# More zero products in the first chain, and other slots for the side units, in a kernel of memory attention followed by a bilinear layer

## The chip, the cores and the metric

The kernel runs on one core of a Trainium2 chip. The metric is the device time of one execution in microseconds (us); the time of a kernel is the median of several executions. Engines are named as in the profile: PE is TensorE, DVE is VectorE, ACT is ScalarE, POOL is GpSimd, SP is SyncE. L337 is line 337 of the kernel.

## What is computed

```python
a   = softmax(phi, axis=seq)                      # (8, 8, 576, 32): batch, heads, seq, memory slots
k_m = einsum('bhsm,bhsd->bhmd', a, k)             # q, k, v: (8, 8, 576, 64)
v_m = einsum('bhsm,bhsd->bhmd', a, v)
attn = softmax(q @ k_m.T / sqrt(64), axis=slots)
x   = (attn @ v_m), heads side by side            # (4608 tokens, 512)
out = ((x @ w_a) * (x @ w_b)) @ w_out             # w_a, w_b: (512, 1536), w_out: (1536, 512)
```

## The kernel before

The eight batches are eight periods of 576 tokens. For each period the kernel folds the memory values into the weights: `vab` holds v_m times w_a and v_m times w_b, for the 8 x 32 memory slots of the heads and the 1536 columns, so that the up projection is one matmul of the attention weights A with `vab`.

A period is made of **side units** and of **up steps**. The side units are made by `units` (L187) and named by short strings:

- `exp0`, `exp1`: exponentials of phi on ACT (L195)
- `qt0` to `qt3`: transposes of q on DVE (L204)
- `ks0`, `ks1`, `vs0`, `vs1`: sums over tokens on PE in tiles of 64 rows and 32 columns (`pk`, L256), then a reciprocal and a scaling on DVE (`kvm`); `kv` and `km` are the same for all at once in later periods (`pkv`, L213; `rep`, L233)
- `kt`, `vt`, `kvt`: transposes on PE and a copy to `kvT` on DVE
- `s0`, `s1`, `sc`: scores on PE (`pscore`, L292); `e0`, `e1`: their exponential E on ACT (L305)
- `den0`, `den1`: denominators on PE (`pD`, L314) and a logarithm on ACT; `nr0`, `nr1`: R on ACT and A = E x R on DVE, from period 3 on on POOL (L325)
- `v0a` to `v2b`: a fold of 512 columns, n = 0, 1, 2, with `w_a` (a) or `w_b` (b) on PE (`pva`, L337); `x0a` to `x2b`: its copies from PSUM, one half on ACT and one on DVE (L349); `hv`, `hx`: the same for 256 columns
- `L`: the four loads of a later period, issued on POOL's queue

An up step is one of 12 blocks of 128 of the 1536 columns: the products `pa` (L584), a copy on ACT (`a_sb`, L587), the products `pb` (L594), and the product `ht` on DVE (L597). A step over both token halves gives a slot after its pa and one after its pb; a half step gives one slot. `ups` (L600) takes the next entry of a list of slots after each. Step i needs only the columns 128 i to 128 i + 127 of `vab`, so steps 8 to 11 alone need the folds v2a and v2b.

The down projection is `po` (L389) for the first four blocks of 128 tokens, which the letters y and a number pull out of `early_downs`, and one level of a Strassen-like scheme after that: `two_downs` (L453) on PE, with sums of ht made on POOL (`h_sums`, L444) and sums of `w_out` (`w_sums`, L429). `Work.advance` spreads these products over the slots by a planned rate.

Periods 0 and 1 begin with a hand-written order, `chain` (L651), which also takes `f` and a number: that many products of zeros of 256 columns (`fill`, L147, into the tile `pw`). The schedule is manual: each engine takes its instructions in the order in which the code issues them. Ahead of everything `fill(16)` runs 16 products of zeros of 512 columns.

The loads are issued on POOL's queue in the order of the code: q, k and v of period 0, then `w_a` and `w_b` in pairs of columns 0 to 256, 256 to 512, 512 to 1024 and 1024 to 1536 (L98), then `w_out`, with the inputs of period 1 between its parts.

Of the kernel before, what the change touches and what calls it, by code (L numbers as in the profile page):

```python
# [18 lines left out]
def kernel(  # L19
# [72 lines left out]
    def load(b):  # L92
        load_phi(b)
        load_k(b)
        load_v(b)
        load_q(b)
# [50 lines left out]
    def fill(n, cols=512):  # L147

        pw = banks.tile([P, 512], F32, name="pw")
        for _ in range(n):  # L150
            nc.tensor.matmul(pw[:, :cols], warm[:, :P], warm[:, :cols], start=True, stop=True)
# [273 lines left out]
    def sum_weights():  # L425
        t = [w_sums[:, x] for x in range(4)]
        for out, in0, in1 in ((t[0], quarter(0, 1), quarter(0, 0)), (t[1], quarter(1, 1), t[0]),
                              (t[2], quarter(1, 1), quarter(0, 1)), (t[3], quarter(1, 0), t[1])):
            nc.gpsimd.tensor_tensor(out=out, in0=in0, in1=in1, op=ALU.subtract)  # L429
# [146 lines left out]
    def up(b, i, hfs):  # L576
        A, vab = attn[b], vabs[b]
        base = S * (b % 2)
        fs = slice(P * i, P * (i + 1))
        a_sbs = []  # L580
        for hf in hfs:
            pa = banks.tile([P, HALF], F32, name="pa")
            for g in range(2):
                nc.tensor.matmul(pa, vab[0][:, g, fs], A[:, g, HALF * hf:HALF * (hf + 1)],  # L584
                                 start=(g == 0), stop=(g == 1))
            a_sb = apool.tile([P, HALF], F16, name="a_sb")
            nc.scalar.copy(out=a_sb, in_=pa)  # L587
            a_sbs.append(a_sb)
        if len(hfs) > 1:
            yield  # L590
        for hf in hfs:
            pb = banks.tile([P, HALF], F32, name="pb")
            for g in range(2):
                nc.tensor.matmul(pb, vab[1][:, g, fs], A[:, g, HALF * hf:HALF * (hf + 1)],  # L594
                                 start=(g == 0), stop=(g == 1))
            t0 = base + HALF * hf
            nc.vector.tensor_tensor(out=ht[:, i, t0:t0 + HALF], in0=a_sbs[hf - hfs[0]], in1=pb, op=ALU.mult)  # L597
        yield

    def ups(steps, side=()):  # L600

        side = iter(side)
        for step in steps:
            for _ in up(*step):
                work.advance()
                next(side, us[step[0]]["-"])()
        for f in side:
            work.advance()
            f()

    def steps(b, lo, hi):

        return [(b, i, (0, 1)) for i in range(lo, hi)]

    def half_steps(b, hf, lo=0):

        return [(b, i, (hf,)) for i in range(lo, NFF)]
# [10 lines left out]
    def slots(b, names):  # L628

        def both(fs):  # L630
            return lambda: [f() for f in fs]
        def unit(n):
            if n == "fin":
                return lambda: work.pull(-work.done % NFF)
            if n == "L":
                return lambda: load(b + 2) if b + 2 < B else None
            if n[0] == "y":
                return lambda: some(int(n[1:]))
            if n[0] == "d" and n[1:].isdigit():
                return lambda: work.pull(int(n[1:]))  # L640
            return us[b + n.endswith("'") - n.endswith("_")][n.rstrip("'_")]

        return [both([unit(n) for n in x.split("+")]) for x in names.split()]
# [3 lines left out]
    def some(n):  # L647
        for _ in range(n):
            next(early, None)

    def chain(b, plan):  # L651


        for x in plan.split():
            if x[0] == "f":
                fill(int(x[1:]), 256)
            elif x[0] == "y":
                some(int(x[1:]))
            else:
                us[b][x]()  # L660

    fill(16)
    chain(0, "exp0 exp1 ks0 kt0 qt0 qt1 f2 s0 e0 ks1 kt1 den0 qt2 qt3 f2 s1 nr0 e1 vs0 vs1 den1 vt0 vt1 nr10 nr11 hv0a hx0a")
    ups(steps(0, 0, 4), slots(0, "hv0b+hx0b hv1a+hx1a - hv1b+hx1b - v1a+x1a - v1b+x1b"))
    load(2)
    ups(steps(0, 4, 12), slots(0, "- - - - v2a+x2a+v2b+x2b - -"))
    chain(1, "exp0 exp1 y9 ks0 y3 kt0 qt0 qt1 y1 y3 ks1 qt2 s0 e0 y6 kt1 qt3 den0 y3 s1 nr0 e1 y4 y2 den1 vs0 vs1 vt0 y1 vt1 nr1 hv0a hx0a hv0b y3 hx0b y2")
    load(3)
    sum_weights()
    ups(steps(1, 0, 4), slots(1, "- hv1a+hx1a hv1b+hx1b+y1 - v1a+x1a y3+v1b x1b y3"))  # L670
    ups(half_steps(1, 0, 4), slots(1, "- v2a+x2a+v2b+x2b+qt0' - - qt1'+exp0'+qt2' exp1' - kv'+km'+y9"))
    work.plan(S + HALF, 10)
    ups(half_steps(1, 1, 4), slots(2, "- kvt qt3 sc+e0+e1+den0 - nr0+den1+v0+x0a - - x0b+nr1 - v1+x1b x1a"))
    second = "v2_+x2a_+exp0 x2b_ exp1 - qt0+kv+km - qt1+qt2 kvt+qt3 sc+e0 - e1+v0+x0a den0+x0b v1+x1a nr0+L x1b+exp0' den1 - nr1+v2+x2a - x2b+exp1' - qt0'+kv'+qt1' km' - qt2'+kvt'+qt3'"
    every = "- sc+e0 e1 den0 v0+x0a+x0b - - nr0+exp0' - - v1+x1a qt0' x1b+den1 exp1' - v2+x2a+x2b nr1+qt1' kv'+km' qt2' - qt3' - kvt'+L -"
    last = "sc+e0 - e1 - v0+x0b - x0a den1 - - den0 v1+x1b x1a+nr0 - - - - nr1+v2+x2a - - - - - x2b"
    for b in range(2, B):
        if b == 2:
            load(4)
# [35 lines left out]
```

The softmax here doesn't subtract the row's maximum and nothing guards it: scores larger than these inputs give would overflow.

## Time and profile before

| What | Value |
|---|---|
| Median of 6 runs | 247.74 us (246.92 to 247.94) |
| Profiled execution, time | 247.71 us |
| Profiled execution, span | 246.0 us |
| PE busy | 232.8 us, 95% |
| DVE, ACT, POOL busy | 168.5, 158.7, 152.9 us |
| Mean granted clock of PE | 0.986 |
| DMA on POOL's queue | 22.71 MB |

The span runs from the first to the last instruction of the program; the time of the execution has 1.7 us more around it. The chain of work that ended last is followed back from the last instruction, at each step to what released it. A busy PE is not PE at its peak: its matmuls are pipelined, and the end of each is modelled, so the step from one start to the next says more than the length of one. The granted clock is 1.00 at full speed. The notation [0.36 <-DMA x] behind an instruction is the idle time of its engine ahead of it, and what ended it.

### The profile page before, as it was taken

How to read it: one execution, taken by the hardware profiler on the slowest of the kernel's cores; microseconds unless marked ns; L12 is line 12 of the kernel's file. 1: busy time of each engine (PE TensorE's matmuls, PEld its weight loads, DVE VectorE, ACT ScalarE, POOL GpSimd, SP SyncE). 2: the span in 40 equal slices, each digit the busy share in tenths (PEclk: the TensorE clock that was granted, in tenths of full speed). 3: DMA queues.
4: the chain of work that ended last, by engine and by line, in shares of the span. 5: the costliest groups of instructions: out<-in, count | busy, mean ns of one | idle time of the engine just before them, and what ended most of it. 6: DMA issues, size and time to landing. Idle time of an engine off the chain costs nothing.

```text
span 246.0 us, 7624 instructions
## 1 busy us (share of the span) xinstructions
PE 232.8 (95%) x3016; PEld 165.4 (67%) x3016; DVE 168.5 (69%) x405; ACT 158.7 (65%) x410; POOL 152.9 (62%) x124
## 2 busy tenths in 40 slices
PE   7769999999998999999999999999999999999992
PEld 2334474456665857767787777877787878888881
DVE  3454884468969968876994659865996586756651
ACT  2364772679697489578856768687956877465430
POOL 8733263499799029892899759892849087946000
PEclk9985999999999999999999999999999999999999
DMA  6999999999979704973159832696120303033153
GB/s 200 209 198 207 209 254 206 256 218 283 224 185 209 160 1 112 233 132 85 32 143 211 180 85 44 165 205 150 38 51 3 85 13 77 19 71 76 44 129 95
DMA packets 26035, 33.81 MB, mean 137 GB/s; under 512 B 1936, under 2 KB 20368, under 8 KB 26000
## 3 DMA queue, kind: packets, MB, share of 16 engines
q0 software_dynamic: 19280, 22.71, 50.4%
q1 hardware_dynamic: 6368, 9.97, 16.4%
q10 hardware_dynamic: 352, 0.66, 0.7%
q8 instruction: 23, 0.38, 0.6%
q14 instruction: 12, 0.10, 0.1%
HBM read 42.47 MB, written 9.44 MB: 211 GB/s over the span
## 4 chain that ended last, share of the span: by engine, by line
PE 82%; DMA 11%; DVE 3%; issue 1%; ACT 1%; POOL 1%; DVEq 0%; POOLq 0%
PE pa L584 19%; PE pb L594 18%; PE py L462 16%; PE pv L462 8%; DMA wb_sb<-in_moe_w_b_dram 7%; PE pva L337 5%; PE po L389 5%; DMA kv_sb<-in_v_dram 4%; PE px L462 4%; PE pkv L213 2%; PE pD L314 2%; PE pscore L292 1%; PE pT L242 1%; PE pk L256 1%; POOL q_sb L90 1%
## 5 line engine op out<-in xcount | busy, mean ns | idle before, releaser
L597 DVE TENSOR_TENSOR ht<-a_sb,pb 128x288 f16<-128x288 f16 x192 | 83.0, 449 | 41.9 <-ACT a_sb L587 28.7
L587 ACT CAST a_sb<-pa 128x288 f16<-128x288 f32 x192 | 75.0, 405 | 31.5 <-PE pa L584 29.3
L584 PE MATMUL pa<-A,vab 128*128 128x288 f16 x384 | 77.4, 291 | 1.5 <-DVE A L325 1.1
L594 PE MATMUL pb<-A,vab 128*128 128x288 f16 x384 | 77.2, 289 | 0.7 <-ACT vab L349 0.5
L444 POOL TENSOR_TENSOR h_sums<-ht 128x768 f16<-128x768 f16 x28 | 45.9, 1640 | 38.7 <-DVE ht L597 37.2
L594 PEld LDWEIGHTS <-vab 128*128 128x128 f16 x384 | 37.5, 99 | 13.4 <-issue 1.7
L584 PEld LDWEIGHTS <-vab 128*128 128x128 f16 x384 | 34.9, 99 | 16.0 <-issue 8.7
L462 PEld LDWEIGHTS <-h_sums 128*128 128x128 f16 x384 | 37.4, 98 | 6.9 <-issue 0.4
L349 ACT CAST vab<-pva 128x512 f16<-128x512 f32 (+1 forms) x52 | 28.1, 558 | 12.7 <-PE pva L337 12.7
L349 DVE CAST vab<-pva 128x512 f16<-128x512 f32 (+1 forms) x52 | 32.7, 644 | 2.9 <-PE pva L337 2.2
L462 PEld LDWEIGHTS <-ht 128*128 128x128 f16 x288 | 28.2, 98 | 5.6 <-issue 0.4
L462 PE MATMUL py<-w_sums,h_sums 128*128 128x256 f16 x192 | 30.3, 272 | 0.0
L444 POOL TENSOR_TENSOR h_sums<-h_sums,ht 128x768 f16<-128x768 f16 x14 | 23.1, 1649 | 1.0
L444 POOL TENSOR_TENSOR h_sums<-ht,h_sums 128x768 f16<-128x768 f16 x14 | 23.0, 1642 | 1.0
L305 ACT ACTIVATE E<-pscore 128x288 f16<-128x288 f32 x32 | 11.4, 416 | 11.3 <-PE pscore L292 11.2
L325 POOL TENSOR_TENSOR A<-E,R 128x576 f16<-128x576 f16 x10 | 12.8, 1275 | 7.0 <-ACT R L323 6.8
L462 PE MATMUL py<-wo_sb,ht 128*128 128x256 f16 x96 | 16.0, 273 | 0.0
L462 PE MATMUL pv<-w_sums,h_sums 128*128 128x256 f16 x96 | 16.0, 273 | 0.0
L469 ACT ACTIVATE u<-py 128x256 f32<-128x256 f32 x32 | 12.4, 388 | 5.2 <-PE py L462 4.9
L462 PE MATMUL py<-w_sums,ht 128*128 128x256 f16 x96 | 15.5, 272 | 0.1
L462 PE MATMUL px<-wo_sb,ht 128*128 128x256 f16 x96 | 15.4, 273 | 0.0
L204 DVE STREAM_TRANSPOSE qT<-q_sb 128x288 f32<-128x288 f32 x32 | 14.3, 461 | 0.6 <-DMA q_sb<-in_q_dram 0.6
(62 smaller groups left out, 261.9 us busy)
## 6 DMA issues: line engine op xcount, KB each, us to landing
out_dram<-o_sb SPq DMA_DIRECT2D x70, 128.0 KB, 2.5
kv_sb<-in_v_dram POOLq DMA_DIRECT2D x7, 576.0 KB, 10.4
phi_sb<-in_phi_dram POOLq DMA_DIRECT2D x7, 576.0 KB, 4.6
kv_sb<-in_k_dram POOLq DMA_DIRECT2D x7, 576.0 KB, 8.7
q_sb<-in_q_dram POOLq DMA_DIRECT2D x6, 576.0 KB, 13.2
wo_sb<-in_moe_w_out_dram POOLq DMA_DIRECT2D x3, 512.0 KB, 16.3
q_sb<-in_q_dram POOLq DMA_DIRECT2D x4, 288.0 KB, 12.7
wa_sb<-in_moe_w_a_dram POOLq DMA_DIRECT2D x2, 512.0 KB, 14.7
```

Source lines behind the costliest of these rows:

```text
L204: nc.vector.transpose(out=t["qT"][:, hp, :].bitcast(F32), in_=qs[b][:, hp, :].bitcast(F32))
L325: engine.tensor_tensor(out=attn[b][:, g, sl], in0=t["E"][:, g, sl], in1=t["R", g][:, sl], op=ALU.mult)
L337: nc.tensor.matmul(t["pva", lo, z][g][0][32 * j:32 * j + 32, 0:hi - lo], t["kvT"][64 * r:64 * r + 64, 4 + g, M * j:M * j + M], w_sbs[z][64 ...
L349: engine_copy(out=vabs[b][z][:, g, lo:hi], in_=pva[:, 0:hi - lo])
L389: nc.tensor.matmul(po, ht[:, i, P * c:P * (c + 1)], wo_sb[:, i, :], start=(i == 0), stop=(i == NFF - 1))
L444: engine.tensor_tensor(out=out, in0=in0, in1=in1, op=op)
L462: nc.tensor.matmul(po, lhs[:, i], rhs[:, i], start=first and i == 0, stop=i == KH - 1, skip_group_check=not first)
L469: nc.scalar.mul(out=x, in_=po, mul=scale)
L584: nc.tensor.matmul(pa, vab[0][:, g, fs], A[:, g, HALF * hf:HALF * (hf + 1)], start=(g == 0), stop=(g == 1))
L587: nc.scalar.copy(out=a_sb, in_=pa)
L594: nc.tensor.matmul(pb, vab[1][:, g, fs], A[:, g, HALF * hf:HALF * (hf + 1)], start=(g == 0), stop=(g == 1))
L597: nc.vector.tensor_tensor(out=ht[:, i, t0:t0 + HALF], in0=a_sbs[hf - hfs[0]], in1=pb, op=ALU.mult)
```

## The change

More products of zeros are put into the first chain: `fill(20)` instead of `fill(16)`, and 32 products of 256 columns in seven places instead of 4 in two. In period 0 the folds v2a and v2b, which were one unit in the fifth slot of `ups(steps(0, 4, 12))`, become two, in the first and the third. In the chain of period 1 the early products y, the transpose qt2 and the unit den1 get other places, and in the slot lists of periods 1 to 7 some units move by one to three slots. No other unit is added, and none is removed. On PE the order differs by the zero products and the moved units; on POOL only one A moves ahead of one `h_sums`, in the last period; SP's order is the same.

```diff
-    fill(16)
-    chain(0, "exp0 exp1 ks0 kt0 qt0 qt1 f2 s0 e0 ks1 kt1 den0 qt2 qt3 f2 s1 nr0 e1 vs0 vs1 den1 vt0 vt1 nr10 nr11 hv0a hx0a")
+    fill(20)
+    chain(0, "exp0 exp1 ks0 f2 kt0 f4 qt0 qt1 s0 e0 ks1 f6 kt1 den0 qt2 qt3 f8 s1 nr0 e1 f2 vs0 vs1 den1 vt0 vt1 f4 nr10 nr11 hv0a hx0a f6")
     ups(steps(0, 0, 4), slots(0, "hv0b+hx0b hv1a+hx1a - hv1b+hx1b - v1a+x1a - v1b+x1b"))
     load(2)
-    ups(steps(0, 4, 12), slots(0, "- - - - v2a+x2a+v2b+x2b - -"))
-    chain(1, "exp0 exp1 y9 ks0 y3 kt0 qt0 qt1 y1 y3 ks1 qt2 s0 e0 y6 kt1 qt3 den0 y3 s1 nr0 e1 y4 y2 den1 vs0 vs1 vt0 y1 vt1 nr1 hv0a hx0a hv0b y3 hx0b y2")
+    ups(steps(0, 4, 12), slots(0, "v2a - x2a+v2b x2b - - -"))
+    chain(1, "exp0 y9 exp1 ks0 y4 kt0 qt0 qt1 qt2 y3 ks1 s0 e0 y6 kt1 qt3 den0 y3 s1 y4 nr0 e1 vs0 den1 vs1 vt0 vt1 y1 nr1 hv0a hx0a hv0b y3 hx0b y5")
     load(3)
     sum_weights()
-    ups(steps(1, 0, 4), slots(1, "- hv1a+hx1a hv1b+hx1b+y1 - v1a+x1a y3+v1b x1b y3"))
-    ups(half_steps(1, 0, 4), slots(1, "- v2a+x2a+v2b+x2b+qt0' - - qt1'+exp0'+qt2' exp1' - kv'+km'+y9"))
+    ups(steps(1, 0, 4), slots(1, "hv1a+hx1a - hv1b+hx1b+y1+y1 - - v1a+x1a+y3 v1b+x1b+y1 -"))
+    ups(half_steps(1, 0, 4), slots(1, "v2a+x2a+v2b+x2b+qt0' - - - qt1'+exp0'+qt2' exp1' - kv'+km'+y9"))
     work.plan(S + HALF, 10)
-    ups(half_steps(1, 1, 4), slots(2, "- kvt qt3 sc+e0+e1+den0 - nr0+den1+v0+x0a - - x0b+nr1 - v1+x1b x1a"))
-    second = "v2_+x2a_+exp0 x2b_ exp1 - qt0+kv+km - qt1+qt2 kvt+qt3 sc+e0 - e1+v0+x0a den0+x0b v1+x1a nr0+L x1b+exp0' den1 - nr1+v2+x2a - x2b+exp1' - qt0'+kv'+qt1' km' - qt2'+kvt'+qt3'"
-    every = "- sc+e0 e1 den0 v0+x0a+x0b - - nr0+exp0' - - v1+x1a qt0' x1b+den1 exp1' - v2+x2a+x2b nr1+qt1' kv'+km' qt2' - qt3' - kvt'+L -"
-    last = "sc+e0 - e1 - v0+x0b - x0a den1 - - den0 v1+x1b x1a+nr0 - - - - nr1+v2+x2a - - - - - x2b"
+    ups(half_steps(1, 1, 4), slots(2, "- qt3+kvt - sc+e0+e1+den0 - nr0+den1+v0+x0a - x0b nr1 - v1 x1b+x1a"))
+    second = "v2_+x2a_+exp0 x2b_ exp1 - qt0+kv+km qt1 qt2+kvt qt3 sc+e0 - e1+v0+x0a den0+x0b v1+x1a nr0+L x1b+exp0' den1 - nr1+v2+x2a x2b+exp1' - - qt0'+kv'+qt1' km' - qt2'+kvt'+qt3'"
+    every = "- sc+e0 e1 den0 v0+x0a+x0b - - nr0+exp0' - - v1+x1a qt0' x1b+den1 exp1' - v2+x2a+x2b nr1+qt1' qt2'+kv'+km' - L qt3' kvt' - -"
+    last = "sc+e0 e1 - - v0+x0b x0a den0 - - den1 - nr0+v1+x1b x1a - - - nr1+v2+x2a - - - - - - x2b"
```

## The prediction

> **What bounds it.** I read the chain of work that ended last first, then the timeline of TensorE (PE), then the waits, then the windows of granted clock. All times are microseconds from the start of the span. On the page the chain is PE for 82% and DMA for 11%; in order of time the DMA part lies wholly ahead of 30.4:
>
> ```profile
> 14.33 16.07 DMA wb_sb<-in_moe_w_b_dram
> 30.40 0.04 issue
> 30.45 0.41 PE pva L337 x8
> 30.86 0.60 PE pb L594 x4
> ```
>
> The columns are start, length and what. The load issued at 14.33 is the last third of `moe_w_b`, columns 1024 to 1536. It lands at 30.40, and the fold `v2b` (L337) starts 0.05 later. The timeline of PE shows how nearly PE was there itself:
>
> ```profile
> 29.09 0.65 PE L584 MATMUL pa<-A,vab 128*128 128x288 f16 x4
> 29.67 0.41 PE L337 MATMUL pva<-wa_sb,kvT 64*32 64x512 f16 x8
> 30.45 0.41 PE L337 MATMUL pva<-wb_sb,kvT 64*32 64x512 f16 x8 [0.36 <-DMA wb_sb<-in_moe_w_b_dram]
> 30.79 0.66 PE L594 MATMUL pb<-A,vab 128*128 128x288 f16 x4
> ```
>
> So PE was free at 30.09 (30.45 less 0.36) and waited for the load. What precedes 30.40 on PE is not on the path: the chain goes into DMA there and comes out only at 3.6. POOL's queue dates the loads, since its next issue waits for a place: the `moe_w_a` half of the same columns lands about 0.3 before 28.16, as the other lands 0.29 before 30.69.
>
> ```profile
> 28.16 0.71 POOL L85 DMA_DIRECT2D kv_sb<-in_v_dram  x1 [1.82 <-DMA wa_sb<-in_moe_w_a_dram]
> 30.69 0.72 POOL L85 DMA_DIRECT2D kv_sb<-in_v_dram  x1 [1.83 <-DMA wb_sb<-in_moe_w_b_dram]
> ```
>
> After 30.8 PE hardly rests until the last stores. Its waits between 36 and 80 are only two, and after that the windows show about 0.08 idle in 85 to 90 and 0.36 in 100 to 110; from 110 to 230 PE is busy 10.00 in every 10.
>
> ```profile
> PE pa L584 <- DVE A L325: 1.1, 1, 1.1
> PE pD L314 <- ACT E L305: 0.5, 1, 0.5
> ```
>
> The clock, last, in windows between the times at which the granted clock changed or could have (second column PE busy, then after four more engines the clock):
>
> ```profile
> 13.78:17.19 3.41, 2.25 (x104) 1.18 (x90) 1.70 (x7) 2.34 (x7) 1.22 (x2) 1.00 1.45 197
> 17.19:20.60 3.41, 2.43 (x23) 1.11 (x16) 1.10 (x4) 1.52 (x4) 1.83 (x4) 0.50 1.33 207
> 20.60:24.02 3.42, 3.42 (x28) 1.57 (x27) 2.27 (x6) 1.48 (x4) 1.37 (x2) 0.50 1.23 203
> 6.95:10.36 3.41, 2.26 (x52) 1.02 (x50) 2.03 (x7) 1.26 (x2) 2.64 (x5) 1.00 1.21 206
> ```
>
> PE ran at half clock for 6.83, from 17.19 to 24.02. That is what zero products could cure. PE was busy 2.43 + 3.42 = 5.85 of it, so a full clock is worth at most half, 2.9, at that place. It is not on the path, because the load at 30.40 comes later anyway.
>
> **Zero products.** Ahead of the first sums, four more of 512 columns. The last of the 16 starts at 7.30 with a step of 0.216, so they end at 7.52, and the sums start at 7.78 when their exponential is there. Four more end at 7.52 + 0.86 = 8.38: the first chain starts 0.60 later. Inside the chain 4 products of 256 columns become 32. A 256-column matmul of L462 steps by 0.109 at full clock, so f2 is 0.22, f4 0.44, f6 0.65, f8 0.87. f2 ahead of kt0 and f6 ahead of kt1 stand in waits for `kvm` of 0.59 each (0 and 0.06 too long); f4 ahead of s0 in the 0.46 for qT (0); f8 ahead of s1 stands where f2 and 0.22 of wait were, 0.43, so 0.43 too long at most; f2 ahead of vs0 has no cover, 0.22; the last f4 and f6 stand in 0.97 and 0.48 of wait, 0 to 0.17. In all the first pa (17.81) comes 1.2 to 1.5 later, and the clock gives back 0 to 2.9 by 24. If that cover were gone, all 28 added products would be 28 x 0.109 = 3.1. Value for the end: 0, hidden behind the load at 30.40; no load is issued by anything that waits for PE there.
>
> **The fold moved ahead.** Here is the loss I expect. The two folds of the last third, v2a and v2b, were one unit behind the pa of step 6. Now v2a stands behind the pa of step 4 and v2b behind the pa of step 5, and PE takes its queue in order. Behind v2b stood 11 products pa or pb; now 13 do, although those two need only weights that are long there. After the landing each takes 0.49 (30.86 to 36.35 in the chain). PE reaches v2b now at 30.09 - 2 x 0.49 = 29.1 plus the delay of 1.2 to 1.5 without the clock (30.3 to 30.6), and earlier with it; so the load still ends last, with 0.2 over at worst. On the way PE waits at v2a until about 27.9 and at v2b until 30.4, instead of doing pb and pa there. The stage that ended at 36.35 ends 2 x 0.49 = **0.98 later**. Queued behind the two waits on PE are only pb and pa, and ACT and DVE wait for these and for nothing else then. Bounds: 0.98 if the load stands, 1.2 with the late reach.
>
> **Chain of period 1.** It is the same 48 early products (0.216 each) in other places: 0. den1 now stands between vs0 and vs1. A change between whole-array products and narrow tiles shows as a step: a pb ahead of a fold takes 0.216 instead of 0.123, and the last of pk ahead of a po 0.148 instead of 0.003. One more such pair: 0.09 + 0.15 = +0.24. qt2 moves ahead of ks1 on DVE, and it waits there for q until 42.65; the sums, kvm and kt1 queue behind it, but y6 (1.30) stands ahead of kt1: 0, and if that cover fails 0.5.
>
> **Periods 1 to 2.** hv1, v1 and y move by a slot where PE has no wait: 0. v2 and its copies go one half step (0.49) ahead. DVE is without a pause from 57.91 to 67.3, and the ends of its ht release POOL's sums at 63.27, so 0 to -0.5, taken -0.2. qt3 ahead of the copy of kvT takes the stretch out of the scores at 66.70 (0.42 from the first to the last start, against 0.21 at 86.52): -0.2. The 1.06 for A at 74.93 stays: A took 1.46 there against 0.46 at 70.36, with POOL's h_sums from 72.89 to 74.56 beside it, and neither order changes. Unshown, it may go or double, so -1.06 to +1.0; I take 0, by the unchanged order.
>
> **Periods 2 to 7.** In `second` kvt comes one slot sooner after kv: two slots of about 0.82 = 1.64 after pkv's end (80.82), and DVE's rep ends at 82.77, 1.95 after: +0.2 (0.1 to 0.3). In `every` four slots or 3.3 remain, over 1.95: 0. In `last` e1, den, nr and v2 move by one to four slots, and PE has no idle time to win from 110 to 230: 0. Load issues (L, 4 x 0.75 on POOL) move three slots ahead, but POOL's queue keeps its order but for one A ahead of one h_sums (1.65) in the last period, where POOL is busy 3.29 of 10: 0. SP's stores keep their order.
>
> **Sum.** 0.98 + 0.24 - 0.2 - 0.2 + 0.2 = +1.0 on the profiled execution's 247.71 (span 246.0 and 1.7 around it; the median of the runs is 247.74, the same here): **248.7**. By its bounds, without the wait for A: 0.98 + 0.24 - 0.5 - 0.2 + 0.1 = 0.6 to 1.2 + 0.24 + 0.5 + 0.3 = 2.2, so 248.3 to 249.9.
>
> **Rivals.** First, the clock falls in the new waits. PE then waits some 1.5 at v2a and 1.2 at v2b between 26 and 30.4, and works some 1.6 in a window of 3.41. For: the clock fell at 17.19 after a window that was busy 2.25, with no pause over 0.97. Against: it stood after a window of 2.26 that held whole-array products, as this one would; the window that lost it held nearly only tiles of 32 columns. Price: one or two windows at half clock from 30.4 on, 1.7 to 3.4 on top: 250.4 to 252, slower. The Trainium skill, "TensorE: Matmul & The Clock Gate", section "What's actually happening", gives the half clock to at least one idle window of about 3.4 us, and so would leave the clock alone in waits of 1.5 and the sum at 248.7. The fall at 17.19, with no pause over 0.97, does not agree with it.
>
> Second, the loss is caught later: the wait of 1.06 for A, or PE's 0.55 for E, takes up most of the 1.0. For: A waits for POOL, ACT and DVE, not for PE alone. Against: all three are themselves fed by PE in 50 to 63. About 247.8, no change.
>
> Third, on the other side: faster. The new places take out the idle that is left, 1.06 + 0.55 + 0.36 + 0.08 + 0.22 (45 to 50) = 2.3, against 0.98 lost: 246.4. It decides from 1.5 removed on, so A's wait must go and half of the rest with it. For: A's 1.46 is an accident of meeting POOL. Against: the rows around it keep their order. That the zero products do not hold the clock belongs to the forecast, since it costs nothing at 30.40.
>
> **Chances.** Forecast (248.3 to 249.9) 0.60; clock falls 0.10; caught later 0.17; faster 0.13. A measurement of this kernel tells about 0.2%, 0.5 us, from no change. Slower 0.60 + 0.10 = 0.70, same 0.17, faster 0.13. The range 247.0 to 250.0 leaves out the falling clock and the larger half of the faster case.
>
> **What will show it.** In the profile after: the load of the last `wb_sb` still lands at 30.4; PE waits for `wa_sb` and `wb_sb` more than 2 in all between 25 and 30.5; 13 pa and pb follow, and the first po starts near 37.2 instead of 36.2; the clock is whole after 30; the wait for A near 75 to 76 is still about 1. I am wrong if the first po is no later than 36.4, or if PE's waits for A, E and rep shrink by over 1.

## The result, and the profile after

| | Before | After |
|---|---|---|
| Median | 247.73 us (36 runs) | 248.82 us (18 runs) |
| Profiled execution, time and span | 247.71, 246.0 us | 248.94, 247.1 us |
| PE busy | 232.8 us | 234.2 us |
| Mean granted clock | 0.986 | 0.998 |
| First `po` starts at | 36.19 us | 37.10 us |

The changed kernel is slower: the ratio of the times is 1.0041, with a 95% interval of 1.0033 to 1.0049. Four of the 18 executions, at 252.2 to 253.6, and one of the 36 of before, at 253.22, are left out of the ratio, and why they took longer is not shown here. The other 14 have a median of 248.68, so +0.95 over before; the profiled execution, which the steps below are told from, has +1.23, and +1.14 of it shows in the starts of the last products.

The chain of the kernel after, in order of time (start, length, what):

```profile
14.06 16.28 DMA wb_sb<-in_moe_w_b_dram
30.34 0.04 issue
30.38 0.41 PE pva L337 x8
...
36.77 0.49 PE pb L594 x4
37.26 1.94 PE po L389 x9
```

It is the same load as before, it lands 0.06 sooner, and from there to the first po (L389) two more products, a pa and a pb, have to pass. The timeline of PE of the kernel after around the two folds:

```profile
26.86 0.67 PE L584 MATMUL pa<-A,vab 128*128 128x288 f16 x4
27.84 0.41 PE L337 MATMUL pva<-wa_sb,kvT 64*32 64x512 f16 x8 [0.32 <-DMA wa_sb<-in_moe_w_a_dram]
28.18 0.66 PE L594 MATMUL pb<-A,vab 128*128 128x288 f16 x4
28.68 0.65 PE L584 MATMUL pa<-A,vab 128*128 128x288 f16 x4
30.38 0.41 PE L337 MATMUL pva<-wb_sb,kvT 64*32 64x512 f16 x8 [1.04 <-DMA wb_sb<-in_moe_w_b_dram]
30.72 0.66 PE L594 MATMUL pb<-A,vab 128*128 128x288 f16 x4
```

PE waits 0.32 and 1.04 in front of weights. Behind the second wait 13 products stand in its queue; the eight of steps 8 to 11 need this fold, the five ahead of them do not, and the change put two of these five there. The first po in the timelines of before and of after:

```profile
36.19 2.10 PE L389 MATMUL po<-wo_sb,ht 128*128 128x512 f16 x9
```

```profile
37.10 2.11 PE L389 MATMUL po<-wo_sb,ht 128*128 128x512 f16 x9
```

From the first product of v2b to the first po it is 5.74 in before and 6.72 in after, 0.98 apart. The waits of PE, whole span (total, times, longest):

```profile
PE pk L256 <- issue: 1.7, 1, 1.7
...
PE pa L584 <- DVE A L325: 1.0, 1, 1.0
PE pD L314 <- ACT E L305: 0.8, 1, 0.8
...
PE pva L337 <- DMA wa_sb<-in_moe_w_a_dram: 0.3, 1, 0.3
```

The wait for A stands at 1.0. New at the top is 1.7 for "issue" in the sums of v, where nothing is named. The windows of the kernel after (length, then PE busy, weight loads, DVE, ACT, POOL, then the clock):

```profile
13.78:17.19 3.41, 2.10 (x85) 1.28 (x83) 1.43 (x4) 1.92 (x5) 1.48 (x2) 1.00 1.45 196
17.19:20.60 3.41, 2.97 (x45) 1.70 (x44) 1.59 (x6) 1.71 (x6) 1.64 (x3) 1.00 1.32 204
20.60:24.02 3.42, 2.83 (x41) 1.61 (x40) 2.19 (x6) 2.11 (x7) 1.30 (x2) 1.00 1.24 207
27.50:31.00 3.50, 2.14 (x28) 1.16 (x28) 1.82 (x4) 2.02 (x7) 1.09 (x2) 1.00 1.25 223
```

The zero products did hold the clock: 1.00 where it was 0.50 from 17.19 to 24.02, and it holds through the new waits too. None of that reaches the end, because the chain is in the load there. The first three stretches are those that the prediction shows for before. In every trace the changes of the clock lie whole multiples of 3.41 apart, and in this one the first is at 7.25, so its own windows are 14.08 to 17.49, with PE busy 1.79, and 27.73 to 31.14, with 2.26; the clock held behind both.

Comparing the starts of the same `pb` products (L594) in the two traces gives the running difference, after less before: +0.91 from 32 to 59, +0.85 at 65, +0.81 at 77, +0.77 at 84, +0.78 up to 124, then three steps of +0.12 near 126, 156 and 181, and +1.14 at the end. The experiments take these apart.

### The profile page after: what moved, and what is told of

It reads as the page before. It is cut to its first block, busy times and chain, and to the rows that moved or that the text cites. A ratio compares the mean times of both kernels' runs of the same rounds, so it can differ in the third digit from the quotient of the medians.

```text
span 247.1 us, 7687 instructions
## 1 busy us (share of the span) xinstructions
PE 234.2 (95%) x3048; PEld 166.9 (68%) x3048; DVE 167.9 (68%) x405; ACT 158.8 (64%) x410; POOL 152.8 (62%) x124
## 4 chain that ended last, share of the span: by engine, by line
PE 82%; DMA 11%; DVE 2%; issue 1%; ACT 1%; POOL 1%; DVEq 0%; POOLq 0%
PE pa L584 19%; PE pb L594 18%; PE py L462 16%; PE pv L462 8%; DMA wb_sb<-in_moe_w_b_dram 7%; PE pva L337 5%; PE po L389 5%; DMA kv_sb<-in_v_dram 4%; PE px L462 4%; PE pkv L213 2%; PE pD L314 2%; PE pscore L292 1%; PE pT L242 1%; PE pk L256 1%; POOL q_sb L90 1%
## 5 line engine op out<-in xcount | busy, mean ns | idle before, releaser
L584 PE MATMUL pa<-A,vab 128*128 128x288 f16 x384 | 76.5, 287 | 1.1 <-DVE A L325 1.0
L594 PE MATMUL pb<-A,vab 128*128 128x288 f16 x384 | 76.0, 286 | 0.6 <-ACT vab L349 0.6
L594 PEld LDWEIGHTS <-vab 128*128 128x128 f16 x384 | 37.1, 98 | 12.5 <-issue 1.4
L315 ACT ACTIVATE L<-pD 128x288 f32<-128x288 f32 x32 | 11.5, 416 | 6.1 <-PE pD L314 6.0
```

The source lines that it names most:

```text
L315: nc.scalar.activation(out=t["L", g][:, sl], in_=pD, func=AF.Ln)
```

## Experiments

### The folds back in the fifth slot, all else as after

```diff
-    ups(steps(0, 4, 12), slots(0, "v2a - x2a+v2b x2b - - -"))
+    ups(steps(0, 4, 12), slots(0, "- - - - v2a+x2a+v2b+x2b - -"))
```

> The changed kernel with the folds v2a and v2b of period 0 back in one unit in the fifth slot; all else stays changed. Theory (13 instead of 11 products behind the load of wb_sb): 0.98 goes, about 247.9, and the first po starts near 36.1 again. Rival (the loss lies in the zero products or in the slots of the later periods): stays near 248.8. If PE comes to the fold late because the zero products delay it, something between, 248.1 to 248.5.

Measured: 248.45 (7 runs), ratio to before 1.0032 (1.0022 to 1.0043). The first po starts at 35.81, 1.29 sooner than in the kernel after: 0.31 of this is an earlier load (the fold starts at 30.07 instead of 30.38), and 0.98 is the two products. So the fold is priced right at its place, but only part reaches the end, since 0.51 is lost in the chain of period 1. DVE's timeline and then PE's in this kernel show where:

```profile
42.42 0.48 DVE L204 STREAM_TRANSPOSE qT<-q_sb 128x288 f32<-128x288 f32 x1 [1.60 <-DMA q_sb<-in_q_dram]
42.82 0.13 DVE L265 RECIPROCAL rphi<-pk 128x1 f32<-128x1 f32 x1
42.98 0.28 DVE L266 TENSOR_SCALAR kvm<-pk,rphi 128x64 f16<-128x64 f32 x1
```

```profile
41.40 1.47 PE L389 MATMUL po<-wo_sb,ht 128*128 128x512 f16 x6
43.32 0.29 PE L274 MATMUL pT<-ident,kvm 128*32 128x128 f16 x8 [0.45 <-DVE kvm L266]
```

The moved qt2 waits 1.60 for q, the reciprocal and `kvm` stand behind it on DVE, and PE's pT (kt1) waits for kvm. This is the "0.5 if that cover fails" of the prediction; in the kernel after the cover holds only because PE is 1.29 later there, while q is in only 0.37 later (42.79 for 42.42). The 247.9 of the theory is missed; the third case has the right number, but not its reason, since PE is at the fold early and waits 0.55 there.

### The fold moved ahead alone, the rest as before

```diff
-    ups(steps(0, 4, 12), slots(0, "- - - - v2a+x2a+v2b+x2b - -"))
+    ups(steps(0, 4, 12), slots(0, "v2a - x2a+v2b x2b - - -"))
```

> The kernel before with nothing but the folds v2a and v2b of period 0 moved to the first and the third slot; no zero products added. Theory: plus 0.98, about 248.7, first po near 37.2, PE waits at v2b until 30.4. Rival (later slots or zero products cost the 1.1): 247.7. Rival (the new waits let the clock fall): half clock after 30 and 249.5 or more.

Measured: 251.52 (4 runs), ratio 1.0165 (1.0147 to 1.0183): plus 3.86, about four times the loss of the whole change. The first po starts at 36.88, +0.69, which is 0.98 less a load that landed 0.29 sooner; this part is as expected, and the clock does not fall after 24.66. The rest is a new wait of PE, and the two other rows, DVE's and POOL's of the same kernel, name its cause:

```profile
53.54 0.54 PE L584 MATMUL pa<-A,vab 128*128 128x288 f16 x3 [2.77 <-DVE vab L349]
```

```profile
48.91 4.24 DVE L325 TENSOR_TENSOR A<-E,R 128x576 f16<-128x576 f16 x1
53.07 0.74 DVE L349 CAST vab<-pva 128x256 f16<-128x256 f32 x2
```

```profile
48.96 0.75 POOL L90 DMA_DIRECT2D q_sb<-in_q_dram  x1
49.72 3.11 POOL L429 TENSOR_TENSOR w_sums<-wo_sb 128x1536 f16<-128x1536 f16 x1
```

The same A in the trace of before:

```profile
48.22 0.45 DVE L325 TENSOR_TENSOR A<-E,R 128x576 f16<-128x576 f16 x1
```

A takes 0.45 there and 4.24 here: it ends 0.32 after POOL's first `w_sums`. The copy of vab stands behind it on DVE, and PE waits for that copy. I had not expected it in any form. The other wait for an A, in period 2, beside `h_sums`, is the same thing in small (1.42 and 1.46).

The Trainium skill, "SBUF — State Buffer", section "SBUF: two separate sides", has a rule for such pairs: an operation of DVE with both inputs in SBUF and one of GpSimd that reads SBUF share a port pair, the one that starts first holds it for its whole length, and the other stands. The 4.24 agrees that it stands for all of it; but by the records A began 0.81 before w_sums, so who counts as first isn't read from the start of a record.

### R in PSUM, on top of the fold alone

```diff
+            if b == 1 and g == 1:
+                for hf in range(hfs.start, hfs.stop):
+                    s1 = slice(HALF * hf, HALF * (hf + 1))
+                    R = banks.tile([P, HALF], F32, "pR")
+                    nc.scalar.activation(out=R, in_=t["L", g][:, s1], func=AF.Exp, scale=-1.0)
+                    nc.vector.tensor_tensor(out=attn[b][:, g, s1], in0=t["E"][:, g, s1], in1=R, op=ALU.mult)
+                return
```

> The kernel with nothing but the fold moved (251.5), but R of period 1, second head group, goes to PSUM in two halves, so that the product A on DVE reads only one operand from SBUF. Theory (A took 4.24 because it stood against POOL's w_sums over SBUF): A takes about 2 x 0.45, the 2.8 of PE's wait goes, 248.7. Rival (A waits for something else, a queue or a semaphore): A still ends at 53, 251.5.

Measured: 249.18 (6 runs), ratio 1.0059 (1.0044 to 1.0074), with the load landing at 30.51 in the profiled execution. DVE and POOL in this kernel:

```profile
49.31 0.81 DVE L328 TENSOR_TENSOR A<-E,pR 128x288 f16<-128x288 f16 x2
```

```profile
49.36 0.75 POOL L90 DMA_DIRECT2D q_sb<-in_q_dram  x1
50.12 3.11 POOL L436 TENSOR_TENSOR w_sums<-wo_sb 128x1536 f16<-128x1536 f16 x1
```

A starts 0.05 ahead of the issue of q, as in the run before it, and takes 0.81 in two halves; PE's wait of 2.8 is gone. It ends at 50.12, as w_sums begins. One operand moved out of SBUF, so the collision is over the reads of both from SBUF. The edit also cuts A in two, and halves that read both inputs from SBUF were not run; but the product ht, of the same size and with one input in PSUM (`pb`), takes 0.45 in the trace of before both in the 65 cases that lie wholly beside a `w_sums` or `h_sums` and in the 60 with POOL idle. The trace loses 0.6 in the chain of period 1, about what the median has over the theory's 248.7: the fold of w_b starts there 0.06 behind the first half of A and its second bank 0.05 behind the second: it seems to wait for the PSUM banks that R now takes, which no run separates.

### Both folds in the first slot, the rest as before

```diff
+    ups(steps(0, 4, 12), slots(0, "v2a+x2a+v2b+x2b - - - - - -"))
```

> The kernel before with both folds of the last third as one unit in the first slot of the eight steps, so 15 products pa and pb stand behind them instead of 11. Theory: 4 x 0.49 = plus 1.96, about 249.7, if PE is there before the load. Rival (the loss is not by the number of products behind the load, but by the split of the folds into two units): at most plus 0.3. Rival (clock falls in a wait of 3 us): 251 or more, with half clock in the trace after 28.

Measured: 255.77 (6 runs), ratio 1.035 (1.0317 to 1.0382). The first po starts at 39.98, +3.79: 0.16 from a later load, 15 - 11 = 4 products or 1.96, and 1.67 from the clock. The windows of this kernel:

```profile
27.64:31.05 3.42, 0.86 (x17) 0.34 (x18) 0.83 (x2) 1.00 (x3) 0.92 (x2) 1.00 1.24 222
31.05:34.47 3.42, 3.42 (x16) 2.08 (x15) 2.35 (x5) 1.41 (x4) 1.54 (x3) 0.50 1.14 280
```

A window with PE busy 0.86 is followed by one at half clock, priced as in the prediction's first rival. The same A as above takes 4.24 again (from 52.01) and adds 2.9. So the falling clock is real: PE waits 0.66 and 2.13 ahead of the two folds here, and the waits of 0.32 and 1.04 in the kernel after were too short for it. The count of products holds as well, 1.96 for four, so the rival that blames the split into two units is out. The other five executions are 0.7 to 3.7 longer than the profiled one (254.46); what they lost beyond it isn't known.

### The zero products alone, the rest as before

```diff
-    fill(16)
+    fill(20)
```

and the chain of period 0 as in the change.

> The kernel before with nothing but the zero products of the change. Theory: they and the clock that they hold end ahead of the load at 30.4, so no change, 247.7 (plus or minus 0.2), with whole clock from 7 on and a fold at 30.4 as before. Rival (the held clock is a gain): 246.5 or less. Rival (their delay of 1.2 to 1.5 reaches the fold): 248.0 to 249.

Measured: 247.76 (11 runs), ratio 1.0007 (0.9994 to 1.0019). The clock is 1.00 throughout from 7.13; the first po starts +0.18, which is the later landing of the load in this execution (30.58 against 30.40). Within this interval zero products are worth nothing here, and cost nothing. That they hold the clock is seen in all six traces with added ones; of the eight traces without, seven lose it at some time between 12 and 20.

### The folds later, in the seventh slot

```diff
+    ups(steps(0, 4, 12), slots(0, "- - - - - - v2a+x2a+v2b+x2b"))
```

> The kernel before with the two folds of the last third as one unit in the seventh slot, behind the pa of step 7, two slots later than before. 9 products pa and pb stand behind it instead of 11. Theory: PE comes to v2b at about 31.1, after the load, so only PE's old wait of 0.36 goes: 247.3 to 247.5. Rival (each slot is worth 0.49 whichever way it moves): minus 0.98, 246.8. Rival (pa of step 8 now waits for its copies): no gain, 247.7 or more.

Measured: 247.70 (12 runs) against 247.81, ratio 0.9995 (0.9985 to 1.0005). In the profiled execution the clock happened to stay whole at 17, and the first po starts at 34.95, 1.24 sooner: 0.26 from an earlier load and 0.98 from two products fewer behind it, with PE there before the load after all. So at this place the first rival is right, each slot is worth 0.49 in this direction too, and the pa of step 8 doesn't wait for its copies. But 0.64 of the 1.24 goes in the chain of period 1 to loads that are not in yet, 0.29 for k and 0.22 for w_out among it; -0.57 is left at the end of that execution, 247.15, and nothing over all runs, so the theory's 247.3 to 247.5 was missed. Going later with the fold pays only when PE is there in time, and what it gains is met by the next loads.

Over the traces in which PE is at v2b before the load and the clock stays whole, the time from the first product of v2b to the first po depends on nothing but the products behind it:

| Products behind v2b | Time | Traces |
|---|---|---|
| 9 | 4.76 | folds late, and with R and zeros (below) |
| 11 | 5.74 | before, folds back, zeros alone, R of period 2 in PSUM (below) |
| 13 | 6.72 | after, fold alone, R in PSUM, and two more on top of after |

### kv', km' ahead of qt2' in `every`

```diff
-    every = "... nr1+qt1' qt2'+kv'+km' - L qt3' kvt' - -"
+    every = "... nr1+qt1' kv'+km'+qt2' - L qt3' kvt' - -"
```

> The changed kernel with kv and km ahead of qt2 in one slot of the list for periods 4 to 6, as they stood before; all else stays changed. Theory (the trace of after slips by 0.12 in each of these three periods, where the first pv of a pair waits for a bank that km has still to read, and qt2 now stands ahead of km on DVE): minus 0.36, 248.45. Rival (the slips come from the earlier kvt or L): stays at 248.8.

Measured: the profiled execution has a span of 246.8 against 247.1, and the three steps of +0.12 are gone: the running difference to before is +0.76 from 84 to the end. PE's timeline of the kernel after, and then of this one, at the first of the three:

```profile
126.10 0.41 PE L594 MATMUL pb<-A,vab 128*128 128x288 f16 x2
126.46 0.49 PE L462 MATMUL pv<-w_sums,h_sums 128*128 128x256 f16 x3
```

```profile
126.08 0.41 PE L594 MATMUL pb<-A,vab 128*128 128x288 f16 x2
126.32 0.49 PE L462 MATMUL pv<-w_sums,h_sums 128*128 128x256 f16 x3
```

The step from pb to pv is 0.36 and 0.24. In the kernel after, qt2's transpose (0.47) stands on DVE ahead of the copies `rep` (L233), which end at 126.32 instead of 126.09, and these give the PSUM bank of `pkv` back (L234). That pv waits for that bank fits the times and the code; it is argued, not shown. The profiled execution took 248.46, as expected; the median of the six is 252.05 (247.78 to 252.90), which misses the 248.45, so the gain rests on that one trace.

### R of period 1 in PSUM, on top of the kernel after

How near is the kernel after to the 4.24? In the traces, the gap by which the second A of period 1 starts ahead of POOL's issue of q, and the time of that A, where both its inputs are in SBUF:

| Kernel | Gap | A took |
|---|---|---|
| fold alone | 0.05 | 4.24 |
| both folds first | 0.05 | 4.24 |
| after | 0.07 | 0.46 |
| km' ahead of qt2' | 0.08 | 0.46 |
| zeros as 32 products (below) | 0.19 | 0.45 |
| zeros alone | 0.37 | 0.45 |
| before | 0.48 | 0.45 |
| after with folds back | 0.50 | 0.46 |
| folds late | 0.94 | 0.45 |

The change has brought A from a gap of 0.48 to one of 0.07, next to the collision. The run is the kernel after with the seven lines above, which take this A out of reach of it:

> The kernel after, with R of period 1, second group, in PSUM, in two halves, instead of in SBUF. The theory for the executions of the changed kernel near 252 to 253: the product A of period 1 starts just after POOL begins its sums of weights and stands until these end, as in the run of the moved fold alone, where it took 4.24. Theory: no execution is above 250.5; the median is 248.8 to 249.4 (the same edit cost about 0.6 in the chain of period 1 beside what it cured in the run before). Rival, they have another cause: as before some one in four lies at 252 or above.

Measured: 249.09 (6 runs, 248.90 to 250.77), ratio 1.007 (1.0049 to 1.0092). The median is in the range of the theory. None of the six is near 252, but one, 250.77, lies above the bound of 250.5, and at 4 in 18 six without one come by chance in (14/18)^6 = 22% of cases, so neither theory nor rival is shown. In the trace the first half of A starts 0.35 ahead of the issue, away from the collision in any case. The edit itself costs 0.61 in the chain of period 1: the fold of w_b there steps 0.59 to the next product instead of 0.30, after a start 0.3 later. Its two banks follow the ends of A's halves by 0.05 each, as in the run above.

### The same zero time in twice as many instructions

```diff
-    fill(16)
+    fill(32, 256)
```

> The kernel before, with 32 products of zeros of 256 columns ahead of everything instead of 16 of 512: the same time of TensorE, and 32 more of its instructions (16 products and 16 weight loads). In the trace of before TensorE pauses 0.97 us in the transposes of v, with nothing named that it waits for; in the trace of after it pauses 1.67 inside the sums of v; both times 446 of its instructions lie ahead. Theory one, the pause stands at a number of instructions (the instructions are not there yet): it moves some 32 instructions ahead in the order of the work, out of the transposes of v and into the sums of v. Theory two, the pause belongs to those transposes or to a moment near 16.5: it stays at the transposes. The time is the same by both, since all of it lies ahead of the load that lands at 30.4: 247.7, within 0.2%.

The trace of this kernel:

```profile
14.06 0.69 PE L256 MATMUL pk<-kv_sb,exp_sb 64*32 64x64 f16 x65
16.50 0.23 PE L256 MATMUL pk<-kv_sb,exp_sb 64*32 64x64 f16 x7 [1.75 <-issue]
```

The pause went into the sums of v, behind the 65th pk, where the count put it: theory one. In the kernel after it stands there too, behind the 59th (1.67), in before in the pT at 16.49 (0.97). It follows the count of instructions, 446 ahead of it (223 products, each with its weight load), and so it does in all 14 traces of this document. Its end does not follow the count: 16.50 here and 16.49 in before. The traces show what the end goes with. Among the DMA packets that they record are some of 16 KB in a queue named "instruction"; the first of them ends at 15.12 in before, 15.15 here and 16.10 in the kernel after, and the pause ends 1.27 to 1.47 behind it in all 14. So PE seems to wait for instructions on their way; which engine's instructions a packet holds isn't recorded, and no run moved one by itself. The time missed: the median of the six executions is 251.95 (247.97 to 253.34). In the profiled one, 247.98, PE is 0.25 to 0.28 later throughout, because the longer pause brings it to the folds only at 30.49, with the load already there. That small delay set A's gap to 0.19.

### R of period 2 in PSUM, on before

The same seven lines as above with `b == 2`.

> The kernel before, but R of period 2, second head group, goes to PSUM in two halves. Theory (A took 1.46 at 73.42 because of POOL's h_sums beside it): the last A ends near 74.0 instead of 74.88, PE's wait of 1.06 shrinks to about 0.2, 246.9. Rival (the wait is set by ACT's R, or the banks taken for R stop PE elsewhere): 247.5 or more.

Measured: 246.89 (6 runs), ratio 0.9969 (0.9958 to 0.9980), as expected. DVE and POOL in the kernel before:

```profile
73.42 1.46 DVE L325 TENSOR_TENSOR A<-E,R 128x576 f16<-128x576 f16 x1
```

```profile
72.89 1.67 POOL L444 TENSOR_TENSOR h_sums<-ht 128x768 f16<-128x768 f16 x1
```

And in this kernel:

```profile
73.25 0.81 DVE L328 TENSOR_TENSOR A<-E,pR 128x288 f16<-128x288 f16 x2
```

```profile
72.83 1.67 POOL L451 TENSOR_TENSOR h_sums<-ht 128x768 f16<-128x768 f16 x1
```

Before, A ends 0.32 after h_sums does, as it did after w_sums in the fold alone. Here its two halves take 0.81 in the midst of h_sums, where it took 1.46; PE's wait of 1.06 is gone, and the running difference goes from -0.07 at 65 to -0.82 at 77 and stays -0.81 to the end. This beats both kernels.

### Together: R of period 2 in PSUM, the folds in the seventh slot, with and without more zeros

With zeros the chain of period 0 is `"exp0 exp1 ks0 g1 kt0 qt0 qt1 g1 s0 e0 ks1 g2 kt1 den0 qt2 qt3 g2 s1 nr0 e1 vs0 vs1 den1 vt0 vt1 g1 nr10 nr11 hv0a hx0a g2"`, where g is a product of zeros of 512 columns.

> The kernel before with three edits: both folds of the last third as one unit in the seventh slot, so that 9 instead of 11 products stand behind the load; R of period 2, second group, in PSUM; and more products of zeros in the first chain, so placed that they end before the folds are reached. By the sum of what was seen: -0.9 for R, and 0 to -0.6 for the later fold when TensorE has a whole clock from 17 on and so reaches it in time: 246.3 to 246.9. Rival, the zeros and the later fold gain nothing, since the loads of period 1 give all of it back: 246.9, as with R alone.

> The same without the added zeros: both folds in the seventh slot and R of period 2 in PSUM. If the clock falls at 17 in an execution, TensorE reaches the folds late and the later slot gains nothing: 246.9 there, 246.3 where it does not fall. So 246.6 to 246.9; if the zeros pay at all, the run with them lies 0.2 to 0.5 below this one, by the rival they are the same within 0.2.

Measured: with zeros 246.39 (6 runs, 245.97 to 247.20), ratio 0.9952 (0.9936 to 0.9967); without 246.61 (5 runs, 246.10 to 246.92), ratio 0.9955 (0.9943 to 0.9967). Both beat before and after; which of the two is better isn't told by these runs, nor whether the later folds add to R of period 2 in PSUM alone, since the intervals overlap. The profiled execution with zeros shows why so little comes of them:

```profile
35.20 2.10 PE L396 MATMUL po<-wo_sb,ht 128*128 128x512 f16 x9
37.85 0.69 PE L256 MATMUL pk<-kv_sb,exp_sb 64*32 64x128 f16 x36 [0.55 <-DMA kv_sb<-in_k_dram]
...
41.73 1.46 PE L396 MATMUL po<-wo_sb,ht 128*128 128x512 f16 x6 [0.24 <-DMA wo_sb<-in_moe_w_out_dram]
```

The first po starts at 35.20 with zeros and at 36.14 without, and the pb at 54 are 0.07 and 0.05 ahead of before: the 0.98 that two products fewer gave with zeros is given back, 0.79 of it in these two waits for k and w_out. Without zeros the clock fell at 18.02, and PE came to v2b only at 31.19. Both spans are 245.2, as with R of period 2 in PSUM alone.

## Why the prediction was right, and where it was not

- **The fold, +0.98**: right. The first po came 0.91 later with a load 0.06 sooner, and 0.98 goes again, apart from the load, when the fold is put back. It is paid in the chain where the prediction put it, behind the load of wb_sb.
- **Zero products, 0**: right, alone too (1.0007). Their delay was mis-sized: the first pa came 2.03 later (19.84 for 17.81), not 1.2 to 1.5. The first sums came 0.84 later, not 0.60, as the clock rose at 7.25 instead of 6.95, and a pause of 0.97, which the estimate left as it was, became one of 1.67. So PE reached the folds later and waited 1.36 for both; the sign "more than 2 in all" failed. PE still came before the load.
- **den1 between vs0 and vs1, +0.24**: wrong. The difference is +0.91 at 44.40 of before and +0.90 at 55. The two switches are there, but units and early products stand in other places around them; no net cost.
- **qt2 ahead of ks1, 0, else 0.5**: both were right, each in its kernel: 0 in the kernel after, 0.51 when the folds are put back.
- **Periods 1 to 2, -0.2 and -0.2, and `second`, +0.2**: -0.13 in sum from 59 to 84. For the single terms there is no run.
- **The wait for A, unchanged**: right, 1.01 for 1.06. Its cause was in the prediction ("an accident of meeting POOL"), but not its price when the other partner is `w_sums`: 4.24 where I had bounded the loss by +1.0. That the changed kernel doesn't pay it is luck: its A starts 0.07 ahead of POOL's issue, and with 0.05 it took 4.24. The sum has no term for it.
- **`every`, 0**: wrong by +0.36. I counted the slots from kv' to kvt' and not the transposes that DVE does between kv' and the end of rep. Moving one behind km' takes all of it away.

The sum was +1.0 and the starts show +0.91 + 0.00 - 0.13 + 0.36 = +1.14, so two errors (0.24 too much, 0.36 too little) met a right main term. That 248.7 is so near to the median of 248.82 is luck in part; the mechanism of the main term is what the runs show. Of the rivals, the falling clock needs a longer wait (0.66 and 2.13 did it, 0.32 and 1.04 did not); the loss caught later did not come in this kernel, though a gain is caught in just that way by the loads of period 1; and the third needed A's wait to go, which the change doesn't touch and R in PSUM does (-0.8).

## What to carry to other kernels

Put an instruction that waits for a load as late in its engine's queue as its first user allows: each product that needs nothing from the load and stands behind it adds its whole step once the load lands. Filling waits of an engine that is itself waiting for a load later on bought nothing here, whatever the clock showed. Before you shift the work by tenths of a microsecond, look for an operation of DVE that takes 0.45 at one place and 1.46 at another: what it meets on POOL decided here, and a shift made it 4.24.

## What was not expected of the hardware

- A tensor_tensor of DVE with both inputs in SBUF took 0.45 alone, 1.42 to 1.49 beside `h_sums` of 1.63 to 1.67, and 4.24 beside the issue of q and `w_sums` of 3.11. With one input in PSUM two halves took 0.81 beside `h_sums`, and 0.81 beside the issue of q.
- When the clock falls. Counted in each trace's own windows of 3.41 up to 34, and with the products on the whole array (128 x 128) counted apart from those on narrow tiles, nine windows at full clock lost it. In these PE was busy 0.86 to 2.26, of it at most 0.81 on the whole array. Every other window at full clock had either 0.82 and more on the whole array, and then 1.79 busy in all was enough (after, 14.08 to 17.49), or 2.30 and more in all (2.41 in the folds late, 13.46 to 16.87, nearly only narrow tiles). So busy time alone doesn't decide, and narrow tiles seem to count for less. This is read from the 14 traces with small margins (0.81 against 0.82), and no run was made to test it.
- PE pauses 0.63 to 1.75 behind its first 223 products in all 14 traces, with nothing named but "issue", until 1.27 to 1.47 after the first 16 KB packet of instructions.
